# A Performer block with an MLP-Mixer: chunk 0's second channel product and chunk 1's first by seven half-size products, with a new instruction order

## The chip, the cores and the metric

One core of one Trainium2 chip runs the whole program. The metric is the time of one execution on the device in microseconds (us); it is given as a median over the runs shown. TensorE is called PE, VectorE DVE, ScalarE ACT, GpSimd POOL, and SyncE, which here only issues DMAs, SP. PEld is the weight load of PE.

## The reference

Eight batches, eight heads, 576 rows, 64 columns per head, so 512 columns in all. First linear attention with 128 random features, then a Mixer block over the attention's output `x`:

```python
def phi(x):
    proj = np.einsum('bhsd,md->bhsm', x, omega)
    sq = np.sum(x * x, axis=-1, keepdims=True) / 2.0
    h = proj - sq
    h = h - np.max(h, axis=-1, keepdims=True)
    return np.exp(h) / np.sqrt(m)
q_p, k_p = (phi(q_s), phi(k_s))
kv = np.einsum('bhsm,bhsd->bhmd', k_p, v)
z = np.sum(k_p, axis=2)
num = np.einsum('bhsm,bhmd->bhsd', q_p, kv)
den = np.einsum('bhsm,bhm->bhs', q_p, z)[..., None] + 1e-06
...
h = np.maximum(xt @ w_tok1, 0.0) @ w_tok2       # over the 576 rows
u = x + h.transpose(0, 2, 1)
h2 = np.maximum(u @ w_ch1, 0.0) @ w_ch2         # 512 -> 1536 -> 512
return (u + h2).astype(np.float32)
```

## The kernel before

**Tiles.** Each batch's 576 rows are cut into 512 rows, which make one chunk (chunks 0 to 7), and a tail of 64; the eight tails together are chunk 8. For a chunk the attention makes key features `kp` (L707, read out by ACT at L562), query features `qp` (L719), the sums over the keys (L763, L770), and the products with the queries (L796, L798), which DVE (L814) or ACT (L812, head by head) scales by the reciprocals `rc` into `x`. The token mix follows (L824, L831, a relu, L844), and DVE adds the result to `x` at L847: that is `u`, with 128 rows on the partitions. For the channel mix it is needed transposed, as `uT`: chunks from 1 on get it by a DMA that transposes, chunk 0 by PE with an identity.

**The two channel products.** The first product of a chunk takes `uT` and `wc1` (512 by 1536) to `r` (after the relu), the second takes `r` and `wc2` (1536 by 512) to the output rows. Each exists in two forms. The plain first product (L1178; L1184 and L1186 for two column blocks of chunk 0) is 12 column blocks of 4 matmuls with 512 columns. The plain second product, used for chunk 0 alone, is the loop at L1212: 4 row blocks of 12 matmuls with 512 columns, to which L1210 adds `u` by 4 identity matmuls of 128 columns; a copy out (L1218, by the helper at L334) and one store for each row block follow. The fast forms cut each operand into four quarters and do with seven products of quarters what eight would do. They need sums of quarters: for the first product sums of the weights (`qT`, `kT`, `sum`, made once) and sums of `uT`, and joins of the results in `r` (`channel_in_fast`, matmuls L1107, joins L1131 on DVE from pieces that ACT or DVE has read out); for the second product the sums `S` of `r`, the weight differences `T` (L496, made once) and reads that add what is already there (`channel_out_fast`, matmuls L989, reads L969). One fast product of one chunk is 84 matmuls with 256 columns. L343 is the helper `tt` for sums on DVE or POOL, L338 and L340 are the relu on ACT and DVE, and L334 is the copy. Before, the first product is fast from chunk 2 on (`FAST_IN = 2`) and the second from chunk 1 on.

**Loads.** Chunks 0 and 1 are loaded as they are (L367, L378, L385, L399), and PE transposes them. From chunk 2 on a DMA of POOL's queue casts the rows into DRAM scratch and SP's transposing DMA brings them in. `wc1` comes in two halves by L473, the first for column blocks 0 to 5, the second for 6 to 11, and `wc2` in two halves by L488, all by DMAs that POOL issues.

**Order.** Nothing is scheduled while the kernel is built: `ORDER` is a list of job numbers, written out by hand, in which each job (a few instructions on one engine, or a DMA) is issued; a negative number stands for that many warm-up matmuls (L1252, minus one) on PE. `SLOT` gives the buffers and `MOVED` the jobs that run on another engine than the one they are declared for. `Planner.turns` (L163 to L180) looks at jobs with `port=True`: where one on DVE follows one on POOL in the order, or the other way round, the first instruction of the later waits for the last of the earlier. Before, the T sums and the `vbd`, `kt_mask` and `vs` of chunks 0 and 1 were not among them.

Of the kernel before, what the change touches and what calls it, by code (L numbers as in the profile page):

```python
# [213 lines left out]
def kernel(  # L214
# [19 lines left out]
    P = 128  # L234
# [8 lines left out]
    RT = ST // 2  # L243
    RA = R + RT
    NPE = 2
    FAST_IN = 2
    SPLIT = ()
    HALVES = ()
    RW = S * 4 // P
# [205 lines left out]
    def clear(t):  # L455
        return lambda: nc.vector.memset(t, 0.0)
# [829 lines left out]
```

## Time and profile before

| | us |
|---|---|
| median of 3 runs | 269.25 (269.13 to 271.19) |
| the profiled execution: its own time | 270.67 |
| its span in the trace | 268.9 |
| PE busy / PEld busy | 257.9 / 190.6 |
| DVE / ACT / POOL busy | 231.7 / 183.0 / 158.9 |

The span is what the trace covers; the 1.8 us beside it lie before the first and after the last instruction. The profiled execution took 1.4 us more than the median. Busy times are those of the span: an engine that is busy for nearly all of it has little room left, but a matmul's busy time includes the part in which the next has already begun, so PE's share says less than the distance from one matmul's start to the next. The granted clock of PE is full throughout.

### The profile page before, as it was taken

How to read it: one execution, taken by the hardware profiler on the slowest of the kernel's cores; microseconds unless marked ns; L12 is line 12 of the kernel's file. 1: busy time of each engine (PE TensorE's matmuls, PEld its weight loads, DVE VectorE, ACT ScalarE, POOL GpSimd, SP SyncE). 2: the span in 40 equal slices, each digit the busy share in tenths (PEclk: the TensorE clock that was granted, in tenths of full speed). 3: DMA queues.
4: the chain of work that ended last, by engine and by line, in shares of the span. 5: the costliest groups of instructions: out<-in, count | busy, mean ns of one | idle time of the engine just before them, and what ended most of it. 6: DMA issues, size and time to landing. Idle time of an engine off the chain costs nothing.

```text
span 268.9 us, 6989 instructions
## 1 busy us (share of the span) xinstructions
PE 257.9 (96%) x2752; PEld 190.6 (71%) x2752; DVE 231.7 (86%) x494; ACT 183.0 (68%) x425; POOL 158.9 (59%) x160
## 2 busy tenths in 40 slices
PE   4999999999999999989999999999999999999993
PEld 2568455454667985768768777897696788888882
DVE  3999978599999998889999999998987898788982
ACT  1997982089885896879988989878865482273400
POOL 8765553061897966987498852745775004927171
PEclk9999999999999999999999999999999999999999
DMA  7999999999999999999999927844350513040144
GB/s 192 199 208 200 205 207 184 175 220 186 240 168 143 175 207 187 121 198 210 175 222 189 240 85 80 119 85 95 105 152 0 80 67 112 0 157 4 41 146 127
DMA packets 81826, 39.72 MB, mean 148 GB/s; under 512 B 64033, under 2 KB 77729, under 8 KB 81601
## 3 DMA queue, kind: packets, MB, share of 16 engines
q0 software_dynamic: 31712, 17.61, 44.7%
q1 hardware_dynamic: 48560, 19.50, 34.7%
q10 hardware_dynamic: 1520, 2.16, 2.3%
q8 instruction: 21, 0.34, 0.5%
q14 instruction: 13, 0.10, 0.1%
HBM read 35.95 MB, written 16.52 MB: 195 GB/s over the span
## 4 chain that ended last, share of the span: by engine, by line
PE 81%; DMA 7%; POOL 6%; issue 2%; DVE 2%; ACT 1%; POOLq 0%
PE bank L989 23%; PE bank L1107 21%; PE bank L1178 7%; PE bank L1212 4%; PE bank L831 4%; PE bank L844 4%; DMA k<-in_k_dram 4%; DMA uT<-u 3%; PE bank L707 3%; PE bank L796 3%; PE bank L763 2%; PE bank L719 2%; POOL S L343 2%; POOL vs L343 1%; POOL uT L343 1%
## 5 line engine op out<-in xcount | busy, mean ns | idle before, releaser
L562 ACT ACTIVATE kp<-bank 128x512 f16<-128x512 f32 x64 | 35.8, 610 | 13.5 <-PE bank L707 13.1
L338 ACT ACTIVATE r<-bank 128x512 f16<-128x512 f32 (+1 forms) x50 | 29.1, 606 | 20.1 <-PE bank L1107 9.9
L989 PEld LDWEIGHTS <-r 128*128 128x128 f16 x384 | 36.9, 98 | 6.8 <-issue 1.0
L562 ACT ACTIVATE qp<-bank 128x512 f16<-128x512 f32 x64 | 36.7, 631 | 2.5 <-PE bank L719 2.4
L740 DVE TENSOR_REDUCE km<-kp 128x8 f16<-128x1024 f16 x32 | 38.1, 1205 | 0.5 <-ACT kp L562 0.5
L343 POOL TENSOR_TENSOR vs<-v,vs 128x512 f16<-128x512 f16 x22 | 23.7, 1082 | 16.0 <-DVE vs L744 5.5
L1107 PE MATMUL bank<-uT,wc 128*128 128x256 f16 x228 | 30.5, 273 | 1.2 <-DMA uT<-u 1.2
L989 PEld LDWEIGHTS <-S 128*128 128x128 f16 x288 | 27.6, 98 | 4.4 <-POOL S L343 0.2
L1107 PEld LDWEIGHTS <-wc 128*128 128x128 f16 x252 | 23.5, 98 | 5.7 <-DMA uT<-u 1.7
L343 POOL TENSOR_TENSOR S<-r,S 128x768 f16<-128x768 f16 x15 | 24.4, 1641 | 4.5 <-DVE vbd L644 3.4
L989 PE MATMUL bank<-T,r 128*128 128x256 f16 x192 | 23.8, 273 | 0.1
L989 PE MATMUL bank<-T,S 128*128 128x256 f16 x192 | 23.6, 273 | 0.0
L989 PE MATMUL bank<-wc,r 128*128 128x256 f16 x192 | 23.4, 273 | 0.0
L812 ACT ACTIVATE x<-bank,rc 128x64 f16<-128x64 f32 x100 | 22.4, 348 | 0.4 <-DVE rc L803 0.4
L343 POOL TENSOR_TENSOR uT<-uT,uT 128x512 f16<-128x512 f16 x10 | 11.6, 1158 | 17.9 <-PE bank L1107 15.8
L338 ACT ACTIVATE r<-r 128x512 f16<-128x512 f16 (+1 forms) x21 | 16.7, 822 | 7.5 <-DVE r L1131 7.5
L1107 PE MATMUL bank<-uT,qT 128*128 128x256 f16 x126 | 21.7, 272 | 0.0
L847 DVE TENSOR_TENSOR u<-x,bank 128x512 f16<-128x512 f16 x28 | 17.8, 680 | 4.3 <-PE bank L844 4.2
L1107 PE MATMUL bank<-uT,kT 128*128 128x256 f16 x126 | 21.4, 273 | 0.0
L1178 PE MATMUL bank<-uT,wc 128*128 128x512 f16 x88 | 20.5, 380 | 0.0
L969 DVE TENSOR_TENSOR o<-u,bank 128x512 f32<-128x512 f16 x28 | 19.0, 677 | 1.8 <-PE bank L989 1.7
L814 DVE TENSOR_TENSOR x<-bank,rc 128x320 f16<-128x320 f32 x44 | 20.0, 477 | 0.4
(158 smaller groups left out, 612.5 us busy)
## 6 DMA issues: line engine op xcount, KB each, us to landing
out_dram<-o SPq DMA_DIRECT2D x11, 512.0 KB, 4.5
q<-in_q_dram POOLq DMA_DIRECT2D x6, 576.0 KB, 9.2
wc<-in_moe_w_ch_dram POOLq DMA_DIRECT2D x4, 768.0 KB, 13.1
k<-in_k_dram POOLq DMA_DIRECT2D x6, 512.0 KB, 9.4
v<-in_v_dram POOLq DMA_DIRECT2D x6, 512.0 KB, 8.9
out_dram<-o SPq DMA_DIRECT2D x6, 256.0 KB, 3.3
r<-in_q_dram POOLq DMA_DIRECT2D x4, 288.0 KB, 7.6
v<-in_v_dram POOLq DMA_DIRECT2D x4, 256.0 KB, 10.8
```

Source lines behind the costliest of these rows:

```text
L338: nc.scalar.activation(out=out, in_=in_, func=AF.Relu)
L343: (nc.gpsimd if eng == "POOL" else nc.vector).tensor_tensor(**kw)
L562: nc.scalar.activation(out=out, in_=in_, func=AF.Exp, bias=0.0, scale=1.0)
L740: nc.vector.reduce_max(out=t_km[place("km", (b, hp))], in_=src_, axis=AX.X)
L812: nc.scalar.activation(out=to[:, j], in_=ps[:, j], func=AF.Copy, scale=rc[:, j : j + 1])
L814: nc.vector.tensor_tensor(out=to, in0=ps, in1=rc.unsqueeze(2).broadcast_to((P, NJ + 1, D)), op=ALU.mult)
L831: nc.tensor.matmul(ps, w1m[:, j, tb * P : (tb + 1) * P], x[:, j, :], start=False, stop=(j == NJ - 1))
L847: nc.vector.tensor_tensor(out=t_u[place("u", b)][:, j, :], in0=t_x[place("x", b)][:, j, :], in1=bank(n), op=ALU.add)
L969: nc.vector.tensor_tensor(out=o, in0=a, in1=ps, op=ALU.add)
L989: nc.tensor.matmul(ps[:, j * DH : (j + 1) * DH], a[:, cb, j * P : (j + 1) * P], w[:, cb, :], start=(bank_of(b, j0) not in held and j == j0 ...
L1107: nc.tensor.matmul(ps[:, n, :], w(a)[:, (2 * m + n) * P : (2 * m + n + 1) * P], x_[:, a], start=(what in ("P1", "P2", "P5") and n == 0 and ...
L1178: nc.tensor.matmul(ps, wc1[:, db, cb * P : (cb + 1) * P], moving(db), start=(db == 0), stop=(db == ND - 1))
```

## The change

`FAST_IN` goes from 2 to 1, so chunk 1's first product takes the fast form; the loop at L1212 goes, so chunk 0's second product does. Chunk 0 has no `u` with rows on the partitions kept for its reads: four of its reads are therefore plain copies, and `rows_into` adds `u` on PE by 20 identity matmuls of 128 columns; where a product is shared by two quarters, one set has a negative identity (`minus16`, made once on DVE). Its output goes in 2 stores in place of 4, in the same layout. The first two heads' keys are read out one head at a time (two jobs in place of one). The T sums, `vbd`, `kt_mask`, `qt_dup` and `vs` now have `port=True` for every chunk. The copy of the transposed `omega` may run on another engine. `ORDER`, `SLOT` and `MOVED` are new in full. Lines of the kernel after are 4 to 23 higher than before (L1009 is the second product's matmul, L1129 the first's, L999 `rows_into`, L347 `tt`, L504 the T sums).

```diff
-    FAST_IN = 2
+    FAST_IN = 1
+    minus16 = sb([P, P], FP16, "minus16")
+    def minus_identity():
+        nc.vector.tensor_scalar(out=minus16, in0=ident16, scalar1=-1.0, scalar2=None, op0=ALU.mult)
+    j_minus = add("DVE", 0.2, -2.0, minus_identity, deps=[j_ident])
...
-        j_T.append(add("DVE", 0.95, KEYS["T"], ..., deps=[*j_wc2, *j_T[-1:]]))
+        j_T.append(add("DVE", 0.95, KEYS["T"], ..., deps=[*j_wc2, *j_T[-1:]], port=True))
...
-            j_ktm = add("DVE", 0.15, kkt + 0.01, kt_mask, ..., port=b >= 2)
+            j_ktm = add("DVE", 0.15, kkt + 0.01, kt_mask, ..., port=True)
-            j_v = add(e_vs, 1.07, ..., vs_, ..., port=b >= 2)
+            j_v = add(e_vs, 1.07, ..., vs_, ..., port=True)
...
+            plain = c == 0 and base
...
-                if e_read == "ACT":
-                    nc.scalar.copy(out=o, in_=ps)
+                if plain:
+                    copy(e_read, o, ps)
                     return
...
+        rest = {1: [(0, 0, ident16)], 3: [(1, 1, ident16)], 5: [(0, 1, ident16), (1, 1, minus16)], 6: [(1, 0, ident16)]}
+        def rows_into(ps, i, e, by):
+            for j in range(2):
+                for d in range(2):
+                    nc.tensor.matmul(ps[:, j * DH + d * P : j * DH + d * P + P], t_uT[place("uT", 0)][:, 2 * i + j, 2 * e + d, :], by,
+                                     start=False, stop=False, skip_group_check=True)
...
+                    for x in rest.get(k, []) if c == 0 else []:
+                        rows_into(ps, *x)
...
-        if fast:
-            channel_out_fast(c, key, jr)
-            return
-        for j in range(NJ):
-            n = ("h4", c, j)
...
+        channel_out_fast(c, key, jr, jt)
 
     for i in range(4):
-        transposes(0, 2 * i, 2 * i + 2, HEAD["kx"][i], ...)
+        for h0 in (0, 1) if i == 0 else (2 * i,):
+            transposes(0, h0, h0 + 1 if i == 0 else h0 + 2, HEAD["kx"][i], ...)
...
 ORDER = [
-    2, 38, 16, 3, 7, 6, 4, 9, 12, 10, 0, -8, 41, 1, 14, 39, 42, 40, 47, 48, 8, 11, 13, 21, 22, 19, 17, 5, 78, 49,
...
+    17, 2, 7, 5, 6, 4, 12, 10, 8, 23, 0, 9, 13, 31, 20, 11, 18, 32, 19, 29, 22, 3, 1, 39, -8, -7, -6, 48, 40, 50,
...
```

POOL issues the loads one after the other, and at the program's head it also makes the 128x128 identity (the two rows `masks.py`). First before, then now (`r` here are buffers for loaded rows, `vt` and `v` the values, `w` the token weights):

```order
L378 DMA r_129<-in_k_dram 64x1x512
L399 DMA vt_93<-in_v_dram 128x1x128
L367 DMA r_129<-in_q_dram 128x1152 x2
masks.py:197 MEMSET S 128x128
masks.py:199 ISA
masks.py:199 AFFINE_SELECT S<-S 128x128
L399 DMA vt_93<-in_v_dram 128x1x128
```

```order
L382 DMA r_130<-in_k_dram 64x1x512
L371 DMA r_130<-in_q_dram 128x1152 x2
L403 DMA vt_94<-in_v_dram 128x1x128
L371 DMA r_131<-in_k_dram 128x1152
masks.py:197 MEMSET S 128x128
masks.py:199 ISA
masks.py:199 AFFINE_SELECT S<-S 128x128
L403 DMA vt_94<-in_v_dram 128x1x128
```

Five DMAs stand ahead of the identity in place of four. Some rows later in the same engine come the channel weights; `v_91` before and `v_92` now are the values of chunk 1, in two halves:

```order
L473 DMA wc_80<-in_moe_w_ch_dram 128x4x768
L399 DMA vt_94<-in_v_dram 128x1x128 x2
L681 COPY qpt_107<-qpt_107 128x8x64
L473 DMA wc_80<-in_moe_w_ch_dram 128x4x768
L488 DMA wc_81<-in_moe_w_ch_dram 128x6x512
L385 DMA v_91<-in_v_dram 128x4x256 x2
L488 DMA wc_81<-in_moe_w_ch_dram 128x6x512
```

```order
L389 DMA v_92<-in_v_dram 128x4x256
L471 DMA S<-in_moe_w_tok_dram 64x256
L371 DMA r_131<-in_q_dram 128x1152
L371 DMA r_131<-in_k_dram 128x1152
L626 COPY T<-mask 128x16
L347 TENSOR_TENSOR T<-vt_94,mask 128x16x64
L389 DMA v_92<-in_v_dram 128x4x256
L403 DMA vt_95<-in_v_dram 128x1x128
L692 COPY qpt_108<-qpt_108 128x8x64
L481 DMA wc_81<-in_moe_w_ch_dram 128x4x768 x2
L403 DMA vt_95<-in_v_dram 128x1x128
L496 DMA wc_82<-in_moe_w_ch_dram 128x6x512 x2
```

Both halves of those values now stand ahead of both halves of `wc1`, and stood behind them.

On DVE the place is chunk 1's attention output (`x_119` before, `x_120` now) and the weight differences `T`. First before, then now:

```order
L814 TENSOR_TENSOR x_119<-bank_69,rc_148 128x5x64
L343 TENSOR_TENSOR kT_89<-wc_80 128x768
L496 TENSOR_TENSOR T<-wc_81 128x1536
L340 TENSOR_SCALAR r_122<-bank_65 128x512
L847 TENSOR_TENSOR u_123<-x_119,bank_69 128x512
L847 TENSOR_TENSOR u_123<-x_119,bank_64 128x512
L847 TENSOR_TENSOR u_123<-x_119,bank_65 128x512
L847 TENSOR_TENSOR u_123<-x_119,bank_67 128x512
L496 TENSOR_TENSOR T<-wc_81,T 128x1536
L496 TENSOR_TENSOR T<-wc_81 128x1536
L334 COPY o_131<-bank_66 128x512
```

```order
L504 TENSOR_TENSOR T<-wc_82 128x1536
L814 RECIPROCAL rc_143<-bank_68 128x5
L504 TENSOR_TENSOR T<-wc_82,T 128x1536
L814 RECIPROCAL rc_144<-bank_64 128x5
L504 TENSOR_TENSOR T<-wc_82 128x1536
L814 RECIPROCAL rc_146<-bank_66 128x5
L504 TENSOR_TENSOR T<-wc_82,T 128x1536
L814 RECIPROCAL rc_147<-bank_65 128x5
L814 RECIPROCAL rc_148<-bank_63 128x5
L825 TENSOR_TENSOR x_120<-bank_66,rc_146 128x5x64
```

Three of the four T sums came behind chunk 1's `x`, two of them behind its `u`; all four now stand ahead of the `x` scales.

On PE the place is the end of chunk 3's token mix for the tails (`64x512`) and the start of the next first product. Before:

```order
L898 MATMUL bank_63<-r_121,w_79 64x512
L898 LDWEIGHTS w_79
L898 MATMUL bank_63<-r_122,w_79 64x512
L1107 LDWEIGHTS wc_80
L1107 MATMUL bank_68<-uT_127,wc_80 128x256
```

and now:

```order
L909 MATMUL bank_68<-r_122,w_80 64x512
L909 LDWEIGHTS w_80
L909 MATMUL bank_68<-r_123,w_80 64x512
L1009 LDWEIGHTS r_130
L1009 MATMUL bank_66<-T,r_130 128x256
```

Before, chunk 3's first product followed at once; now 24 matmuls of chunk 2's second product, 4 matmuls for queries (2 with 256 columns, 2 with 512) and 18 for keys come between.

More of the change, by code (lines that the diff above doesn't have):

```diff
@@ L129 @@
+    1398: "ACT", 1399: "ACT", 1408: "DVE", 1419: "DVE", 1429: "DVE", 1431: "ACT", 1433: "POOL", 1435: "POOL",
+    1437: "POOL", 1438: "POOL", 1439: "POOL", 1456: "ACT", 1462: "POOL", 1463: "POOL", 1464: "POOL", 1468: "DVE",
+    1480: "ACT", 1484: "DVE", 1495: "ACT", 1496: "ACT", 1500: "DVE", 1505: "DVE", 1512: "ACT", 1514: "POOL",
+    1516: "POOL", 1520: "POOL", 1549: "ACT", 1550: "SP", 1551: "POOL", 1552: "POOL", 1553: "ACT", 1554: "SP",
+    1559: "ACT", 1560: "SP",
 }
@@ L501, with om_out @@
                 deps=[j_om16, j_ident], take=[("bank", "om")])
-    j_omT = add("DVE", 0.2, -9.0, lambda: nc.vector.tensor_copy(out=omT, in_=bank16("om")[:, 0:P]), deps=[j_omt], give=[("bank", "om")])
+    e_omT = engine("DVE")
+    def om_out():
+        copy(e_omT, omT, bank16("om")[:, 0:P])
+    j_omT = add(e_omT, 0.2, -9.0, om_out, deps=[j_omt], give=[("bank", "om")])
     def rows_of(b, w):
@@ L649, in kt_mask @@
                 )
-            j_ktm = add("DVE", 0.15, kkt + 0.01, kt_mask, deps=[j_ktm, j_msk], take=take_vbd, give=[("kmt", b)], port=b >= 2)
+            j_ktm = add("DVE", 0.15, kkt + 0.01, kt_mask, deps=[j_ktm, j_msk], take=take_vbd, give=[("kmt", b)], port=True)
             def vbd():
@@ L970, in read @@
             return add(e_read, 0.345 * (j1 - j0), key + KEYS["c2"] + step * k, go, deps=deps, take=[o_tag(i)],
-                       give=([("bank", bank_of(b, j0))] if free else []) + ([("u", c)] if base and c < B else []))
+                       give=([("bank", bank_of(b, j0))] if free else []) + ([("u", c)] if base and 0 < c < B else []))
         def late_base(k, i, e, x, deps):
@@ L1170, in channel_mix @@
         jr = [None] * NCB
-        fast = c >= NPE - 1
-        order = [x for i in range(NH) for x in (i, i + NH)] if fast else range(NCB)
+        order = [x for i in range(NH) for x in (i, i + NH)]
         for pos, cb in enumerate(order):
```

99 lines of the change are left out of this document (37 added, 62 removed), and 148 rows, old and new, of the table ORDER.

## The prediction

> **What bounds the kernel now.** I read the shares first, then the chain that ended last, then the stretches.
>
> ```profile
> PE 257.9 (96%) x2752; PEld 190.6 (71%) x2752; DVE 231.7 (86%) x494; ACT 183.0 (68%) x425; POOL 158.9 (59%) x160
> PE 81%; DMA 7%; POOL 6%; issue 2%; DVE 2%; ACT 1%; POOLq 0%
> 20.00:40.00 20.00, 20.00 (x245) 12.24 (x242) 17.61 (x41) 17.28 (x41) 10.09 (x13) 1.00 1.25 204
> 40.00:60.00 20.00, 20.00 (x176) 10.13 (x171) 15.60 (x32) 7.61 (x20) 6.59 (x9) 1.00 1.20 198
> 60.00:80.00 20.00, 20.00 (x186) 10.92 (x185) 18.51 (x46) 17.59 (x41) 13.42 (x14) 1.00 1.07 199
> 80.00:100.00 20.00, 20.00 (x249) 17.14 (x247) 19.18 (x43) 16.05 (x44) 16.64 (x17) 1.00 1.16 174
> 100.00:130.00 30.00, 27.97 (x323) 21.02 (x321) 26.22 (x55) 24.46 (x61) 22.65 (x22) 1.00 1.28 185
> 130.00:160.00 30.00, 30.00 (x339) 21.94 (x338) 28.63 (x60) 26.46 (x68) 23.24 (x22) 1.00 0.95 182
> ```
>
> The first two lines are the busy shares and the chain by engine. The six rows are stretches: length, then busy time of PE, PEld, DVE, ACT and POOL, then clock, DMA share and GB/s. PE is on 81% of the chain and busy without a gap in 20 to 100 us; only 100 to 130 lacks 2 us. So PE work that is saved early shortens the run, as long as PE then finds something ready. But DVE is busy 17.61 + 15.60 + 18.51 + 19.18 + 26.22 + 28.63 = 125.75 of the 140 us from 20 to 160. It has 14.25 us to spare, 5.89 of them in 40 to 80, where both changed products run. The question is whether a saving on PE survives a second engine that is nearly full.
>
> **PE: the products.** The distance between matmuls comes from runs of one line in the chain (start, us, line, count):
>
> ```profile
> 43.39 2.59 PE bank L1212 x12
> 53.10 0.22 PE bank L1210 x4
> 60.07 4.42 PE bank L1178 x20
> 76.30 1.31 PE bank L989 x12
> 128.47 3.95 PE bank L1107 x36
> L989 PEld LDWEIGHTS <-r 128*128 128x128 f16 x384 | 36.9, 98 | 6.8 <-issue 1.0 <-DVE r L340 0.2
> ```
>
> A 512-column matmul takes 2.59 / 12 = 0.216 us (4.42 / 20 = 0.221), a 256-column one 1.31 / 12 = 0.109 (3.95 / 36 = 0.110), an identity matmul 0.055. Each of the two products loses 48 x 0.216 = 10.37 us and gains 84 x 0.109 = 9.16: 1.21 saved, twice 2.42. The residual takes 20 identity matmuls for 16, +0.22. PE's sum is **-2.2 us**. Two more warm-up matmuls lie in PE's idle head and count nothing; without that cover they cost 0.43.
>
> The weight loads, 98 ns each in the last row, seem to speak against it: 168 in place of 96. But 12 products with 12 loads of their own take 1.31 us, so the loads run beside the matmuls. Here the Trainium skill has a rule against the change: "TensorE: Matmul & The Clock Gate", section "Measured speedup vs the span model", says that a weight load overlaps a running matmul only where the two use different row groups, and these use all rows. By that rule each half-size matmul would take 109 + 98 ns and each full one 216 + 98, the two products 168 x 0.207 - 96 x 0.314 = +4.6 us in place of -2.42; the 1.31 us row disagrees, as 12 would take 2.48.
>
> **PE: two waits at 100 and 117 us.** Start, length, line, count, and the idle time before it with its releaser:
>
> ```profile
> 101.37 0.29 PE L599 MATMUL bank<-omT,kT 64*128 64x128 f16 x4 [0.70 <-DMA kT<-k]
> 115.58 0.62 PE L898 MATMUL bank<-r,w 128*64 128x512 f16 x4
> 117.41 0.61 PE L1107 MATMUL bank<-uT,wc 128*128 128x256 f16 x4 [1.21 <-DMA uT<-u]
> ```
>
> At 117.41 the first product of chunk 3 waits 1.21 us for its transposed `u`, right behind L898. In the new order 24 matmuls of the second product (2.6 us at 0.109), 4 for queries (0.65) and 18 for the key sums come between, over 3.2 us. Unless `u` itself is that much later, the wait goes: -1.21, bounds 0 and -1.21. The 0.70 is a transposing DMA that waits on the loads; the order moves its use back a little, so I take half, -0.35, bounds -0.70 and +1.21 (as long a wait as the other transposing DMA's). Together **-1.56**. Late next is DVE, below.
>
> **The head.** PE's first work waits for the identity that POOL makes after its DMA issues:
>
> ```profile
> 2.74 1.14 POOL L367 DMA_DIRECT2D r<-in_q_dram  x2
> 4.16 0.29 POOL masks.py:199 TENSOR_SCALAR_AFFINE_SELECT S<-S 128x128 f32<-128x128 f32 x1
> 4.51 1.11 PE L518 MATMUL bank<-S,wc 128*128 128x128 f32 x4 [2.71 <-POOL S masks.py:199]
> ```
>
> L518 begins as soon as the identity is there. Five issues in place of four stand ahead of it now, so it comes one issue of L367 later, 1.14 / 2 = **+0.57** (bounds 0, if ACT's chain from the first keys sets the head anyway, and 0.57). Reading out the first keys one head at a time lets ACT begin earlier by at most one of its pieces, 0.6 us, but it then has one more instruction; I give it nothing.
>
> **The weights' landing.** All these loads stand in POOL's queue.
>
> ```profile
> L473 POOL DMA_DIRECT2D wc<-in_moe_w_ch_dram x2: 757/780/804, 14.0 to 18.6; - x2
> DMA to landing us min/median/max: 11.4/11.6/11.9
> 27.72 2.76 PE L1178 MATMUL bank<-uT,wc 128*128 128x512 f16 x12
> v<-in_v_dram POOLq DMA_DIRECT2D x4, 256.0 KB, 10.8
> ```
>
> The two halves of `wc1` are issued at 14.0 and 18.6 and land 11.4 to 11.9 us later, at about 25.9 and 30.0. The first product starts at 27.72. In the new order two value loads of 256 KB stand ahead of both: 524 KB at the 204 GB/s of the row for 20 to 40 is 2.6 us, so they land near 28.5 and 32.6, earlier issue or not, since bandwidth and not issue holds them back. The first half is then needed at 28.3; the fourth column block, which needs the second half, is about 3 us of PE work later, near 31.4. One wait of at most 1.2 us, some of it already in the start of the head: I take **+0.8**, bounds 0 and +2.6. `wc2` lies behind both in either order and keeps its place.
>
> **DVE, ACT and POOL.** The counts are those of the program's order, the durations those of the rows:
>
> ```profile
> L1131 DVE TENSOR_TENSOR r<-r,bank 128x512 f16<-128x512 f32 x21 | 14.0, 678 | 1.6 <-PE bank L1107 1.3 <-ACT r L334 0.2
> L969 DVE TENSOR_TENSOR o<-o,bank 128x512 f32<-128x512 f32 x21 | 14.0, 675 | 0.9 <-PE bank L989 0.8
> L340 DVE TENSOR_SCALAR r<-bank 128x512 f16<-128x512 f32 x11 | 7.4, 678 | 2.4 <-PE bank L831 1.8 <-PE bank L1178 0.4
> L340 DVE TENSOR_SCALAR r<-r 128x1024 f16<-128x1024 f16 x12 | 5.2, 459 | 0.1
> L343 DVE TENSOR_TENSOR S<-S,r 128x768 f16<-128x768 f16 x14 | 7.7, 553 | 0.2
> L814 DVE TENSOR_TENSOR x<-bank,rc 128x320 f16<-128x320 f32 x44 | 20.0, 477 | 0.4
> L812 ACT ACTIVATE x<-bank,rc 128x64 f16<-128x64 f32 x100 | 22.4, 348 | 0.4 <-DVE rc L803 0.4
> L496 DVE TENSOR_TENSOR T<-wc 128x1536 f16<-128x1536 f16 x2 | 1.9, 949 | 0.0
> L343 POOL TENSOR_TENSOR S<-r,S 128x768 f16<-128x768 f16 x15 | 24.4, 1641 | 4.5 <-DVE vbd L644 3.4 <-DVE S L343 0.6 <-DVE r L340 0.5
> L343 POOL TENSOR_TENSOR vs<-v,vs 128x512 f16<-128x512 f16 x22 | 23.7, 1082 | 16.0 <-DVE vs L744 5.5 <-DMA v<-in_v_dram 3.4 <-DVE r L343 2.4
> ```
>
> DVE gains 9 joins x 0.678 = 6.1, 3 adding reads x 0.675 = 2.0, 4 relus of 1024 from buffers x 0.459 = 1.8 and 6 of 512 at half of that, 1.4, 4 more copies out of PSUM at the joins' 0.68 = 2.7, and 8 sums of `uT`, of `r` and of weights at 0.553 = 4.4. It loses 8 relus from PSUM x 0.678 = 5.4, 5 `x` scales x 0.477 = 2.4 that go to ACT, 2 `vs` that go to POOL and five other copies at 0.68 (4.8). Net 18.4 - 12.6, about **+6 us** of DVE work, nearly all between 20 and 100 us. ACT gains 25 pieces of `x` x 0.348 = 8.7, and its copies gained and relus lost about cancel; the 12.4 us that it has free in 40 to 60 hide that, and without this cover the relus would come later by as much. POOL gains 4 sums net at 1.64 and 2 `vs` at 1.08, 8.7 us; it was busy 6.59 of 20 in 40 to 60: hidden too. The four T sums, contiguous now, stand ahead of chunk 1's five `x` scales. That chunk's `u` thereby comes 3 x 0.95 us later in DVE's order than it would, which is what the freed scales (2.4) about give back. What of the +6 reaches PE is bounded by 0 (the 5.89 us idle in 40 to 80 takes all) and +6 (the idle stays where it is, in front of work that PE releases). I take 0 for the likeliest, because the row for 40 to 60 is the emptiest of all, and the price stands in the rival below.
>
> **Turns.** The waits between DVE and POOL now hold in chunks 0 and 1 too. Behind a waiting T sum stand the `x` scales and so `u`; behind a waiting POOL sum stand the DMA issues for later chunks.
>
> ```profile
> L343 POOL TENSOR_TENSOR vs<-v,vs x22: 1056/1061/1496, 36.8 to 196.8; 128x512 f16<-128x512 f16 x22
> L343 POOL TENSOR_TENSOR T<-vt,T 128x1024 f16<-128x1024 f16 x1 | 1.9, 1922 | 0.7 <-DVE T L644 0.7
> ```
>
> Without turns a POOL operation was stretched by 1496 - 1061 = 0.44 us at most; with them a T sum may wait for a whole POOL product, 1.92. Bounds -0.44 and +1.9; I take **+0.44**, the nearer row. The Trainium skill, "SBUF — State Buffer", section "Who interferes with whom", says that a DVE operation with two SBUF inputs and a POOL operation that reads SBUF exclude each other for the whole instruction in any case: by that a turn would cost nothing but the choice of who goes first, 0 in place of 0.44. The stretch to 1496 agrees with some exclusion, and is shorter than a whole one.
>
> **The sum.** On the profiled execution: 270.67 - 2.20 - 1.56 + 0.57 + 0.80 + 0.44 = 268.72. That execution was 1.42 above the median, so 267.3.
>
> **The rivals.**
>
> *DVE becomes the bound* (slower). Place: 40 to 80 us, DVE at 34.11 of 40 before. If the idle time sits in front of instructions that PE releases, it cannot be filled, and two thirds to all of the 6 us (4 to 6) reaches PE: 271.3 to 273.3, middle 272.3. It decides from where DVE is busy over 39 of those 40 us. For it: 19.18 of 20 already in 80 to 100, so nothing is made up there. Against: PE has work of two other chunks to put in between, and ACT has 12 us free. Chance 0.25.
>
> *All is recovered*: both waits go (-1.91), the head and the landing cost nothing: 270.67 - 2.20 - 1.91 = 266.56, less 1.42 gives 265.1. For it: a new order can place what I priced as waits behind other work. Against: DVE. Chance 0.23.
>
> *The landing takes it*: the second half of `wc1` costs the full 2.6: 269.1, no change. For it: 204 GB/s is as much as the queue moves in any stretch here. Against: 3 us of column blocks come first. Chance 0.08.
>
> *The weight loads bind*, so that the change does not do what it says: 270.67 + 4.6 + 0.22 - 1.42 = 274.1. Against it the 1.31 us row. Chance 0.02.
>
> **How the numbers follow.** The likeliest, **267.3 us**, has 0.42 and 265.7 to 269.0 of its own. One per cent, 2.7 us, is about what a measurement of this kernel can tell from no change, as the three runs spread over 2.1. Below 266.56 lie 0.17 of the forecast and all of the recovery, 0.40; above 271.9 lie two thirds of the DVE rival and the weight loads, 0.18; between them 0.42. The range from 264.4 to 272.4 leaves out the better end of the recovery and the worse half of the DVE rival, under 0.2 together.
>
> **What would show it.** Each fast product as runs of 12 at 1.31 us, in chunks 0 and 1 too; L518 near 5.1 us; no wait of the first product behind L909; the first column block of the first product starting within 28 to 29 us. DVE over 39 of 40 us in 40 to 80, with PE waiting for DVE's joins or `x`, would show the rival. The forecast is wrong if PE gets gaps before 100 us, which it had none of, or if the waits at 100 to 120 only move to another chunk.

## The result and the profile after

| | us | to before on the same chip |
|---|---|---|
| after, median of 4 runs | 273.04 (272.92 to 273.18) | 1.0126 [1.0077, 1.0176], before 269.57 |
| after, again on another chip | 273.63 | 1.0167 [1.0126, 1.0209], before 269.35 |
| profiled execution, before and after | 270.67 and 273.02 | span 268.9 and 271.2 |

The change is slower by 1.3 to 1.7%. Forecast were 267.3 us and 264.4 to 272.4. Here and below the medians hold every execution, and the ratios leave out those that took over 1.5% longer than the fastest of the same kernel (one each of h3 and h5, two of h4).

The shares and the chain by engine, then the stretches as in the prediction (length, busy PE, PEld, DVE, ACT, POOL, clock, DMA share, GB/s), of after:

```profile
PE 260.8 (96%) x2830; PEld 199.5 (74%) x2830; DVE 236.2 (87%) x509; ACT 190.1 (70%) x456; POOL 166.8 (61%) x166
PE 89%; ACT 4%; DVE 3%; POOL 2%; issue 1%; POOLq 0%; DVEq 0%
20.00:40.00 20.00, 19.56 (x254) 12.20 (x252) 16.49 (x42) 17.94 (x46) 9.90 (x13) 0.93 1.24 209
40.00:60.00 20.00, 19.91 (x215) 13.43 (x215) 18.71 (x41) 13.32 (x38) 8.43 (x7) 1.00 0.98 147
60.00:80.00 20.00, 19.91 (x238) 15.27 (x239) 19.16 (x47) 19.12 (x49) 14.90 (x18) 1.00 1.07 198
100.00:130.00 30.00, 30.00 (x353) 22.98 (x351) 28.98 (x63) 24.64 (x57) 23.35 (x25) 1.00 1.14 173
```

Three things are new: PE is no longer full in 20 to 100 us, its clock was 0.93 in 20 to 40, and 100 to 130 is full. DVE went from 34.11 to 37.87 of the 40 us from 40 to 80.

Busy shares hide how much PE loses, so I took every matmul's start from the trace. A matmul of this kernel needs 0.216 us for 512 columns, 0.109 for 256 and some 0.056 for 128 at full clock, by the rows of the prediction. For one with 64 rows I count half of that and for one in f32 twice; this is a way of counting, not a measurement, and as both kernels have equally many of these it cancels in the differences. What the distance to the next start has beyond that is **lost time**: waiting, or a slow clock. By stretch, in us:

| | before | after | h3 | h8 | t2 |
|---|---|---|---|---|---|
| PE's own work | 244.9 | 243.2 | 242.8 | 242.8 | 243.2 |
| lost, 0 to 40 | 10.5 | 15.2 | 11.2 | 11.5 | 14.1 |
| lost, 40 to 100 | 1.8 | 3.6 | 8.9 | 5.8 | 3.4 |
| lost, 100 to 130 | 3.5 | 1.4 | 1.4 | 1.3 | 1.6 |
| lost, later | 2.7 | 2.9 | 3.2 | 2.9 | 2.9 |

The last three columns are experiments below. For after against before: -1.7 + 4.7 + 1.8 - 2.2 + 0.2 = +2.8 up to the start of the last matmul; what follows it is 0.45 shorter, and 2.35 is the 2.3 us by which the spans differ. PE got what was promised, 1.7 of work and 2.2 of waits, and lost 6.5 in the first 100 us. The 4.7 up to 40 us divide into -0.6 up to 14 us, +4.1 from 14 to 24 and +1.3 from 24 to 40.

**The products.** Pieces of after's chain (start, us, what):

```profile
33.08 1.02 PE bank L1199 x4
47.99 2.78 PE bank L1009 x24
53.16 1.48 PE bank L1009 x12
56.37 1.31 PE bank L1009 x12
```

The half-size matmuls keep their distance of 0.109 us (1.31 / 12) in chunk 0 too. But the first product starts at 33.08 in place of 27.72, and the second product of chunk 0 at 47.99 in place of 41.91. What follows this second start takes 223.2 us of the span in after and 227.0 before: the change loses 6.1 us ahead of it and gains 3.8 behind it.

**The waits at 100 and 117 us.** PE's instructions in order of time, after:

```profile
116.70 0.62 PE L909 MATMUL bank<-r,w 128*64 128x512 f16 x4
117.26 1.48 PE L1009 MATMUL bank<-T,r 128*128 128x256 f16 x12
```

Nothing waits behind L909 now; at 100 us no idle time is left either. That is not shown to be the new order's doing: in h2 and p1 below, which have before's order there and a span 7 and 3 us longer, PE waits for neither DMA either. Coming later was enough.

**The head.** PE's clock in stretches of 2 us (columns as above), the first two rows of before, the others of after; then three pieces of after's chain and one row each of its ACT and PE:

```profile
16.00:18.00 2.00, 1.87 (x35) 1.25 (x34) 2.00 (x6) 2.00 (x5) 1.12 (x2) 1.00 1.19 211
20.00:22.00 2.00, 2.00 (x40) 1.94 (x37) 1.85 (x9) 1.69 (x7) 2.00 (x3) 1.00 1.12 205
14.00:16.00 2.00, 0.95 (x17) 0.29 (x9) 1.10 (x3) 2.00 (x7) 1.77 (x2) 1.00 1.30 201
16.00:18.00 2.00, 1.38 (x14) 0.68 (x14) 1.88 (x6) 2.00 (x6) 1.75 (x3) 1.00 1.26 203
18.00:20.00 2.00, 1.87 (x25) 1.22 (x23) 1.75 (x3) 2.00 (x6) 0.76 (x2) 0.81 1.32 206
20.00:22.00 2.00, 2.00 (x13) 0.90 (x11) 1.05 (x4) 1.75 (x5) 2.00 (x3) 0.50 1.12 206
22.00:24.00 2.00, 1.91 (x42) 1.57 (x40) 1.65 (x6) 1.30 (x7) 1.84 (x4) 0.83 1.41 185
```

```profile
5.02 1.11 PE bank L529 x4
12.65 1.20 PE bank L1249 x5
20.05 1.71 PE bank L1249 x4
13.88 0.62 ACT L622 ACTIVATE kpt<-bank,kt_nb 128x128 f16<-128x128 f32 x2 [1.44 <-PE bank L1249]
16.08 0.28 PE L680 MATMUL bank<-qT,omT 64*128 64x256 f16 x2 [0.67 <-ACT qT L338]
```

The identity comes at 5.02, as forecast (before 4.51). What is late lies behind it: of the five warm-up matmuls at 12.65 one goes into the bank that holds the scores of the tails' keys, and ACT's exp of them waits 1.44 us for it. PE then finds work for only 0.95 and 1.38 of 2 us, its clock stands at half for 3.4 us (the rows from 18 to 24 show its parts), and four warm-up matmuls that should take 4 x 0.216 = 0.86 us take 1.71 in the chain. Every wait of PE between 14 and 18 us is for ACT; the longest is the last row above. Before, ACT is busy for all 12 us from 8 to 20; in after it is busy for 10.05 of them, and its idle time lies before 14. So PE follows ACT there, and ACT has lost some 2 us by 14. How much of the time the halved clock costs is open: one of the four executions of after had the full clock throughout and took 273.18 us, no less than the others.

**DVE ahead of chunk 1's `u`**, in order of time, after:

```profile
43.71 0.95 DVE L504 TENSOR_TENSOR T<-wc 128x1536 f16<-128x1536 f16 x1
46.66 0.92 DVE L504 TENSOR_TENSOR T<-wc,T 128x1536 f16<-128x1536 f16 x1
48.78 1.68 DVE L825 TENSOR_TENSOR x<-bank,rc 128x320 f16<-128x320 f32 x4
52.09 1.01 DVE L347 TENSOR_TENSOR S<-S,r 128x768 f16<-128x768 f16 x2
55.19 2.48 DVE L858 TENSOR_TENSOR u<-x,bank 128x512 f16<-128x512 f16 x4
```

The four T sums (the first and last are shown) fill 43.7 to 47.6, the scales follow, then the sums `S` for the second product, then `u`. PE hardly waits for this in after, because its own second product comes so late.

### The profile page after: what moved, and what is told of

It reads as the page before. It is cut to its first block, busy times and chain, and to the rows that moved or that the text cites. A ratio compares the mean times of both kernels' runs of the same rounds, so it can differ in the third digit from the quotient of the medians.

```text
span 271.2 us, 7205 instructions
## 1 busy us (share of the span) xinstructions
PE 260.8 (96%) x2830; PEld 199.5 (74%) x2830; DVE 236.2 (87%) x509; ACT 190.1 (70%) x456; POOL 166.8 (61%) x166
## 4 chain that ended last, share of the span: by engine, by line
PE 89%; ACT 4%; DVE 3%; POOL 2%; issue 1%; POOLq 0%; DVEq 0%
PE bank L1009 30%; PE bank L1129 26%; PE bank L842 5%; PE bank L855 5%; PE bank L774 3%; PE bank L1199 3%; PE bank L718 3%; PE bank L807 3%; PE bank L730 3%; PE bank L529 1%; PE bank L1249 1%; PE bank L835 1%; ACT qp L573 1%; PE bank L893 1%; PE bank L895 1%
## 5 line engine op out<-in xcount | busy, mean ns | idle before, releaser
L1009 PEld LDWEIGHTS <-r 128*128 128x128 f16 x432 | 41.4, 98 | 7.9 <-issue 1.6
L1129 PE MATMUL bank<-uT,wc 128*128 128x256 f16 x264 | 36.3, 273 | 0.0
L1009 PEld LDWEIGHTS <-S 128*128 128x128 f16 x324 | 31.1, 98 | 5.8 <-issue 0.7
L347 POOL TENSOR_TENSOR vs<-v,vs 128x512 f16<-128x512 f16 x24 | 25.0, 1056 | 13.0 <-DVE r L344 5.5
L823 ACT ACTIVATE x<-bank,rc 128x64 f16<-128x64 f32 x125 | 28.3, 345 | 3.3 <-DVE rc L814 3.3
L1129 PEld LDWEIGHTS <-wc 128*128 128x128 f16 x288 | 27.5, 98 | 3.7 <-issue 0.2
L347 POOL TENSOR_TENSOR S<-r,S 128x768 f16<-128x768 f16 x16 | 26.0, 1642 | 4.2 <-DVE S L347 4.1
L1009 PE MATMUL bank<-T,r 128*128 128x256 f16 x216 | 26.9, 273 | 0.0
L1009 PE MATMUL bank<-T,S 128*128 128x256 f16 x216 | 26.5, 273 | 0.0
L1009 PE MATMUL bank<-wc,r 128*128 128x256 f16 x216 | 26.4, 273 | 0.1
L1129 PE MATMUL bank<-uT,qT 128*128 128x256 f16 x144 | 25.3, 273 | 0.0
L1129 PE MATMUL bank<-uT,kT 128*128 128x256 f16 x144 | 25.0, 273 | 0.0
L347 POOL TENSOR_TENSOR r<-r 128x768 f16<-128x768 f16 x10 | 16.3, 1638 | 11.5 <-DVE r L347 9.6
L338 ACT COPY qp<-bank 128x512 f32<-128x512 f32 x21 | 12.4, 600 | 11.1 <-PE bank L1129 10.0
L1153 DVE TENSOR_TENSOR r<-r,bank 128x512 f16<-128x512 f32 x24 | 16.2, 676 | 2.4 <-PE bank L1129 2.0
L347 POOL TENSOR_TENSOR uT<-uT 128x512 f16<-128x512 f16 x9 | 10.4, 1155 | 12.7 <-DVE r L344 12.7
```

Source lines behind the costliest of these rows:

```text
L347: (nc.gpsimd if eng == "POOL" else nc.vector).tensor_tensor(**kw)
L823: nc.scalar.activation(out=to[:, j], in_=ps[:, j], func=AF.Copy, scale=rc[:, j : j + 1])
L1009: nc.tensor.matmul(ps[:, j * DH : (j + 1) * DH], a[:, cb, j * P : (j + 1) * P], w[:, cb, :], start=(bank_of(b, j0) not in held and j == j0 ...
L1129: nc.tensor.matmul(ps[:, n, :], w(a)[:, (2 * m + n) * P : (2 * m + n + 1) * P], x_[:, a], start=(what in ("P1", "P2", "P5") and n == 0 and ...
L1153: nc.vector.tensor_tensor(out=r3(i, j, m), in0=kept(what, m).rearrange("p (n t) -> p n t", n=2), in1=pair(b, m), op=ALU.add)
```

## The experiments

Most kernels here are after (or before) with a stretch of the other's order of jobs, buffers and engines put in; where two orders meet (the seam), new waits can arise, and I name them. The head is the program's start, up to chunk 0's first or second product; "old head" is before's order.

**The head alone, both ways.** h1 has before's order on all engines up to the first product, then after's; h2 is before with after's order up to there. POOL's loads, h1 against after:

```diff
-v_92 (chunk 1's values, first half), ..., v_92 (second half), ..., wc_81 x2, ..., wc_82 x2
+wc_81, vt_95 x2, COPY qpt, wc_81, wc_82, v_92 x2, wc_82
```

> The kernel after, but every job up to chunk 0's first channel product in the order, on the engines and in the buffers of before (identity, loads, transposes, chunk 0's attention and token mix); from there on the order of after. Theory 'head': the loss arises before the first L1199 (27.72 us before, 33.08 after), by PE waits and a lower clock there, and the rest of the new order keeps its gains: first product near 28 us, 268.0 to 269.5 us in all. Rival 'DVE is the bound' (40 to 80 us, DVE 37.9 of 40 busy after): an earlier head is lost in waits behind DVE, 271.5 to 273.

> The kernel before (plain products in chunk 0 and chunk 1 as they were), but every job up to chunk 0's first channel product in the order, on the engines and in the buffers of after. Theory 'head': first product near 33 us, 273 to 275 us. Rival 'DVE is the bound': before's DVE has 5.9 us free in 40 to 80 and takes the late head in, 269.5 to 271.

Measured: h1 277.43, 1.0306 [1.0254, 1.0359]; h2 278.38, 1.0332 [1.0274, 1.0390]. Both were slower than either parent. In h1 the first product started at 30.01, but one DVE row shows what the seam did:

```profile
35.35 0.69 DVE L359 TENSOR_TENSOR vs<-v,vs 128x512 f16<-128x512 f16 x1 [6.83 <-DMA v<-in_v_dram]
```

After's later order needs chunk 1's values early, and before's loads bring them late. In h2 the first product started only at 37.45, later than in either parent. Neither run says what the head alone is worth.

**The same without that seam.** x1 keeps after's order on POOL (two halves of chunk 1's keys exchanged) and has before's order on the other engines up to the first product; x2 is h1 with chunk 1's values ahead of `wc1` and the halves of `wc1` exchanged.

```diff
 DMA r_131<-in_q_dram 128x1152
+DMA v_92<-in_v_dram 128x4x256 x2
 DMA wc_81<-in_moe_w_ch_dram 128x4x768
 ...
-DMA v_92<-in_v_dram 128x4x256 x2
```

> The kernel after; PE, DVE, ACT and SP work through chunk 0's token mix stands in the order, on the engines and in the buffers of before, POOL's loads stand as after (but the two halves of chunk 1's keys change places), and the rest is the order of after. The first run of this kind lost 4.1 us where DVE waited at 35 us for chunk 1's values, which the old load order brings late; here they come early. Theory 'head': first product near 28.5 us, 268.0 to 270 us in all. Rival 'DVE is the bound': 271.5 to 273.

> As the run with the old head, loads in the old order too, but chunk 1's two value loads moved ahead of the channel weights, and the two halves of wc1 exchanged, as after has them. The identity then stands behind four DMA issues as before. Theory 'head': no wait of DVE at 35 us, 267.5 to 270 us; the identity 0.5 us earlier than in the other run with old compute order. Rival 'DVE is the bound': 271.5 to 273. If the weights' landing is what counts: the first product starts late, near 29 to 30, with PE waiting for wc, and the time is 270 to 272.

Measured: x1 275.96, 1.0258 [1.0218, 1.0297]; x2 273.95, 1.0190 [1.0156, 1.0224]. The first product started at 34.93 and 33.66. In x1 PE waits 1.35 us for DVE's `vs` (18.41) and 2.06 us for a load of keys (23.35). In x2, POOL and PE:

```profile
16.94 0.74 POOL L493 DMA_DIRECT2D wc<-in_moe_w_ch_dram  x1 [1.43 <-DMA r<-in_k_dram]
20.20 0.62 POOL L704 COPY qpt<-qpt 128x512 f16<-128x512 f16 x1
20.88 0.20 PE L821 MATMUL bank<-kvsb,qpt 128*128 128x65 f16 x1 [2.33 <-POOL qpt L704]
```

POOL's DMA issues wait here until earlier transfers have landed (1.43 us in the first row), and a copy that PE needs stands behind them. In h1, where the two loads stand later, the copy runs at 17.44 and PE has no such wait: two loads moved forward cost PE 2.33 us through POOL, not through their landing. So the head is a balance of loads and ACT, DVE and POOL work, and half of one does not go with half of the other.

**The warm-ups.** w1 puts the fifth matmul into another bank; w2 leaves the five out.

```diff
-    138, 122, 100, 42, 43, 15, 84, -2, -2, -2, -2, -4, 66, 74,
+    138, 122, 100, 42, 43, 15, 84, -2, -2, -2, -2, -2, 66, 74,
```

> The kernel after with one number of the order changed: the last of the five warm-up matmuls at 12.6 us goes into bank 1, as the four before it, in place of bank 3, whose key scores for the tails L622 has yet to read. Theory 'head': ACT's wait of 1.44 us at 13.88 goes, its work up to the first product comes earlier by most of it, PE idles less in 14 to 18 us and the clock drops for a shorter time: 270.5 to 272. Rival 'DVE is the bound': 273, no change.

> The kernel after without the five warm-up matmuls at 12.6 us. ACT's wait goes as with the other bank, but PE has 1.1 us less work in the stretch after which its clock was halved (18.8 to 22.7 us). Theory 'head', with the idle PE as the cause of the low clock: the clock drops as early or earlier, and the time is 0.3 to 1 us above that of the run with the other bank, 271 to 273. If the clock has another cause: the same as with the other bank or better, 270.5 to 272.

Measured: w1 272.56, 1.0107 [1.0067, 1.0146]; w2 273.13, 1.0135 [1.0092, 1.0178]. In w1 the clock stayed at 1.00, in all six executions. In w2 it was at half for 6.8 us:

```profile
18.00:20.00 2.00, 2.00 (x16) 0.53 (x12) 1.91 (x5) 1.95 (x6) 2.00 (x3) 0.50 1.34 207
```

By the ratios w1 is 0.5 us faster than the first run of after and 1.6 faster than the second; the intervals overlap, so the bank and the halved clock together cost at most something like this. The starts of the first product say no more: 32.70 in w1 and 34.07 in w2, but 33.08 and 34.30 in the two profiled executions of after itself, since a load of keys made PE wait up to 1.4 us near 9 us in some executions and not in others. What the five warm-ups are worth in time is not shown.

**The turns.** n1 takes `port=True` away from the T sums, `qt_dup` and the `vbd`, `kt_mask` and `vs` of chunks 0 and 1.

```diff
-  ... deps=[*j_wc2, *j_T[-1:]], port=True))
+  ... deps=[*j_wc2, *j_T[-1:]]))
-  ... give=[("v", b)], port=True)
+  ... give=[("v", b)], port=b >= 2)
```

> The kernel after with the flag for turns as before: the T sums, vbd, kt_mask, qt_dup and vs of chunks 0 and 1 take none. If the turns cost what was put down for them, 0.4 us: 272.6. If they are part of the loss in the head: POOL's wait of 2.0 us for DVE at 35.8 and the like go and 271 to 272 comes out. If they save contention: 273.0 to 273.6.

Measured 276.01, 1.0254 [1.0199, 1.0308], so by 0.9 to 1.3% slower than after by the ratios, though its interval overlaps that of after's second run: the turns cost nothing that shows. One T sum took 2.28 us here and POOL's S sums 2.23 on average, where after has 0.96 and 1.63. But the loss is not there: the second product starts at 50.30, and what follows takes 223.5 us, against 223.2 in after. It lies in the head, and whether the turns or the chance of the loads made it is not shown.

**Everything up to chunk 0's second product as before.** h3 has before's order up to there and after's behind it, where PE's late start cannot hide DVE; h4 is before with after's order up to there. h3 against after, on DVE: before's head, and the T sums behind only two of the five `x` scales of chunk 1.

```diff
+TENSOR_TENSOR x_120 x2
 TENSOR_TENSOR kT, qT x2
 TENSOR_TENSOR T x4
-TENSOR_TENSOR x_120 x5
+TENSOR_TENSOR x_120 x3
```

> The kernel after, with everything up to chunk 0's second product in the order, on the engines and in the buffers of before, and everything from there on (both fast products, the new order) as after. The traces put the second product's start at 41.9 us before and 48.0 after, and what follows at 227.0 and 223.2 us of span. Theory 'head': 42 to 43 plus 223 to 225, that is a span of 265 to 268 and 267 to 270 us, below before. Rival 'DVE is the bound' in 40 to 100 us: it cannot use the earlier start, 271.5 to 273.5.

> The kernel before (plain products), with everything up to chunk 0's second product in the order, on the engines and in the buffers of after, and everything from there on as before. Theory 'head': 48 plus 227, 275 to 277 us. Rival 'DVE is the bound': the later start is taken in by DVE's free 5.9 us, 269.5 to 271.5.

> The kernel after once more, on the same chip as the other runs of this call, to compare them with: 272.5 to 273.5 us.

Measured: h3 275.49, 1.0228 [1.0194, 1.0261]; h4 280.79 and 284.95 in the two executions that the ratio counts, 1.0502 [1.0428, 1.0577]; after 273.63, 1.0167 [1.0126, 1.0209]. The profile of h4 is of an execution of 538.85 us and isn't read. In h3, PE and DVE:

```profile
43.94 2.78 PE L1030 MATMUL bank<-wc,r 128*128 128x256 f16 x24
50.32 0.39 PE L856 MATMUL bank<-x,w1t 64*128 64x512 f16 x2 [3.38 <-DVE x L846]
47.66 0.95 DVE L525 TENSOR_TENSOR T<-wc,T 128x1536 f16<-128x1536 f16 x1
48.89 1.28 DVE L846 TENSOR_TENSOR x<-bank,rc 128x320 f16<-128x320 f32 x3
```

The second product starts 4 us earlier than in after, and PE then waits 3.38 us for `x`, which stands behind the T sums. Behind that wait the clock stands at half for 3.4 us (51.0 to 54.4), about 1.7 us more. The lost time moved from before 40 us (15.2 to 11.2) to behind it (3.6 to 8.9), and what follows the second product's start takes 228.5 us in place of 223.2. So there is a second bound right behind the head. With the late head and after's order behind it, it never shows: in the second run of after, w1, w2, n1, t2, x1, x2 and h1, where that start lies between 46.89 and 51.22, the rest takes 223.2 to 223.5 us.

**Moving the T sums.** t1 is after with the T sums behind chunk 1's scales; h5 is h3 with them there and four weight sums behind the S sums; h6 is h5 with two T sums ahead of the S sums, two behind, and without their turn; h7 is h6 with two copies of output and one scale on ACT. p1 is the other way round: before, with all four T sums ahead of the last four scales.

```diff
 (t1, h5)
-TENSOR_TENSOR T x4
 TENSOR_TENSOR x_120 ...
+TENSOR_TENSOR T x4
 TENSOR_TENSOR S
 (p1)
+TENSOR_TENSOR T x4
 TENSOR_TENSOR x_119 x4
-TENSOR_TENSOR T x4 (one here, two behind u, one later)
```

> The kernel after with one edit: the four T sums stand behind chunk 1's last x scale on DVE in place of ahead of the scales. Theory 'two bounds': the scales come 3.7 us earlier, but PE gets to the second product only at 48 because of the head, and no more than 0.5 us is gained: 272.5 to 274. Theory 'the row of T sums is the cause by itself': 270 to 271.5.

> The kernel after with everything up to the second product as before, as in the run that gained nothing by it, and on DVE besides the four T sums and four weight sums moved from ahead of chunk 1's last three x scales to behind them (the weight sums behind the S sums). There PE waited 3.5 us at 46.7 for those scales. Theory 'two bounds, one behind the other' (a late head, and DVE's row of T sums ahead of x): both are gone, the wait at 46.7 too, a span of 266 to 269 and 268 to 271 us. Theory 'head alone' or 'DVE's amount of work alone': DVE has as much to do as before the move, 272 to 275.5.

> The kernel before with one edit: the four T sums stand ahead of chunk 1's last four x scales on DVE, as the new order has them. PE's first matmul of the token mix (45.98 us) needs those scales and stands in front of PE's other work; they come up to 3.7 us later. Theory 'two bounds': 271.5 to 273.5. If DVE or PE make it up later: 269 to 270.

> As the run with the old order until the second product and the T sums behind the x scales, where PE then waited 4.9 us at 49 for the S sums, because POOL's two S sums stood waiting (5.1 us) for their turn behind the T sums. Here the T sums take no turn, and only two of the four stand ahead of the S sums. Theory 'two bounds and the turn': POOL's S sums run from 44.6 to 47.9 beside the T sums, PE's wait falls to 1 us or less, 270.5 to 272.5 us. Theory 'DVE's amount of work' (DVE has no idle time from 39 to 61 us in any order): a wait of PE as long turns up at the next thing that DVE makes, 274 to 276.5.

> The same, with two copies out of chunk 0's second product and one x scale given from DVE to ACT (which is idle for 6 of 10 us there): 1.8 us less work on DVE in 44 to 60 us. Theory 'two bounds and the turn': the same time as without it, within 0.7 us. Theory 'DVE's amount of work': 1 to 1.8 us shorter than without it.

Measured: t1 282.70, 1.0480 [1.0431, 1.0528]; h5 276.52, 1.0242 [1.0199, 1.0285]; p1 273.52, 1.0123 [1.0088, 1.0157]; h6 275.70, 1.0272 [1.0242, 1.0302]; h7 278.85, 1.0392 [1.0372, 1.0411]. One row each of PE in p1 and h5, of POOL and PE in t1, and of POOL and DVE in h6:

```profile
48.66 0.39 PE L821 MATMUL bank<-x,w1t 64*128 64x512 f16 x2 [2.68 <-DVE x L811]
54.08 2.31 PE L1030 MATMUL bank<-T,S 128*128 128x256 f16 x10 [4.90 <-DVE S L368]
56.05 3.22 POOL L345 TENSOR_TENSOR S<-r 128x768 f16<-128x768 f16 x2 [12.02 <-DVE minus L458]
60.86 1.46 PE L1007 MATMUL bank<-T,S 128*128 128x256 f16 x6 [5.96 <-DVE S L345]
44.92 3.24 POOL L368 TENSOR_TENSOR S<-r 128x768 f16<-128x768 f16 x2
46.56 2.43 DVE L525 TENSOR_TENSOR T<-wc 128x1536 f16<-128x1536 f16 x1
```

p1 is the cleanest: nothing of before is changed but the place of the T sums, PE waits 2.68 us for `x`, its clock then stands at half for 3.4 us (49.2 to 52.6, about 1.7 us more), and the kernel is 3.3 us slower by the ratio and 4.1 by the medians, about as much as by the whole change. Behind the scales they do no better: in h5 and t1 POOL's S sums get their turn only after them, and PE waits 4.90 and 5.96 us for S in place of `x`. Without the turn (h6) the sum that meets POOL's S takes 2.43 us. h7 has PE's `T,S` product at 50.70 in place of 51.58, but one of the copies then stood behind other work of ACT, and this cost more than it gained, so it shows nothing on the amount of DVE's work.

**Leaving the T sums out**, with the old head (h8, else h3) and with the new one (t2, else after): the four sums are not computed, and slices of the weights stand in their place. Four kernels make a square of head and T sums.

```diff
-    T1, T2, T3, T4 = [t_T[:, i] for i in range(4)]
+    T1, T2, T3, T4 = W12, W22, W22, W21
-  add("DVE", 0.95, KEYS["T"], lambda o=out_, a=a, b=b: nc.vector.tensor_tensor(...), ..., port=True)
+  add("DVE", 0.95, KEYS["T"], lambda: None, ...)
```

> The kernel after with everything up to chunk 0's second product in before's order (as in h3), and with the four T sums left out: slices of the weights stand in for them, so the operands of every fast second product that would be T are not computed. Theory of two bounds (the head is 5 to 6 us late, and behind it DVE has about 6 us of work more ahead of chunk 1's u): with the early head it is DVE that is late, so the 3.8 us of T sums show: PE's wait of 3.5 us ahead of chunk 1's query weights shrinks to under 1.5, chunk 1's products start at least 3 us earlier than in h3, and the time is h3's 275.5 less 3 to 5, 270.5 to 272.5. Head alone (only the late head matters, DVE fills anyway): no change from h3, 275 to 276. DVE amount alone: h3 less 3.8, and the same 3.8 in t2.

> The kernel after as it is, with the four T sums left out in the same way (slices of the weights stand in for them). Theory of two bounds: with the late head the second product's start and not DVE sets the time, so less comes back than in h8: after's time less 0 to 1.5, 272 to 273.6. DVE amount alone (the second engine is full in 40 to 80 us, whatever the head does): after less about 3.8, 269.5 to 270.2, that is no slower than before by more than half a per cent. Head alone: no change from after, 273 to 274.

Measured:

| | with T sums | without |
|---|---|---|
| new head | 1.0126 [1.0077, 1.0176] and 1.0167 [1.0126, 1.0209] | 1.0180 [1.0135, 1.0225], 273.84 us |
| old head | 1.0228 [1.0194, 1.0261], 275.49 us | 1.0071 [1.0040, 1.0102], 270.92 us |

With the old head the T sums cost 1.57% of 269 us, 4.2 us; with the new one nothing that shows. The traces agree: what follows the second product's start takes 228.5 us in h3 and 225.0 in h8, but 223.2 in after and 223.3 in t2. The stretch from 40 to 60 us, h3 and then h8:

```profile
40.00:60.00 20.00, 16.08 (x164) 11.00 (x163) 17.73 (x39) 6.69 (x20) 10.32 (x10) 0.91 0.97 145
40.00:60.00 20.00, 17.71 (x196) 12.34 (x194) 17.33 (x40) 9.87 (x27) 14.45 (x15) 1.00 1.25 172
```

PE does 32 matmuls more there, and its clock is 1.00 in place of 0.91: about 1.7 of the 4.2 us are the clock that fell behind the wait. That is two bounds, one behind the other, and neither DVE's amount alone (the gain would be the same in both rows) nor the head alone (there would be none). Without the T sums the head by itself is worth the step from 1.0071 to 1.0180, 2.9 us. But h8 still loses 4.0 us more than before in 40 to 100, without any T sum.

**One half of the change.** k1 keeps chunk 0's second product plain and before's order to its end; chunk 1's first product is fast, and the rest is after's.

```diff
-        channel_out_fast(c, key, jr, jt)
+        if c == 0:
+            for j in range(NJ): ...   # the plain loop of before
+            return
+        channel_out_fast(c, key, jr, jt)
```

> One half of the change alone: chunk 0's second product stays plain (48 matmuls of 512 columns, copies, four stores) and everything up to its end keeps before's order, so three T sums stay behind chunk 1's x scales as before and the fourth goes behind chunk 1's first joins; chunk 1's first product is fast, and from there on the order is after's, turns included. Theory of two bounds (the head, and the T and S sums ahead of chunk 1's u): neither bound is touched here, so PE keeps 1.21 us of the one fast product and the 2.2 us of the two waits between 100 and 130 us, less up to 1 us of new waits where the two orders meet: 266 to 268 us, ratio 0.985 to 0.997. Theory that any added DVE work before 100 us reaches PE (9 joins and 6 halves of relu, some 7 us, are still there): PE gets gaps of 2 us or more between 55 and 80 us and the time is 269.5 to 272. Theory that the new turns cost: no better than before, without such gaps.

Measured 278.44, 1.0369 [1.0341, 1.0397]: far from the expectation. DVE's last output copy waited for PE until 59.73, and behind it, in after's order, stood weight sums, a maximum and the tails' adds, before the `uT` sums that the fast product needs at 67.01; PE lost 11.1 us in 40 to 100. That is the seam's doing in good part, so the run doesn't show what half of the change is worth with an order of its own. It does show again that the fast form puts several short DVE operations between `uT` and its first useful matmul, and that they wait behind whatever is ahead of them. No kernel tried was faster than before.

## Why the prediction was wrong

- **PE's sum, -2.2.** Right: -1.7 measured, in which the two extra warm-ups (0.43) count as work; they lie in the wait for the identity, as forecast.
- **The weight loads.** They did not bind: 12 half-size matmuls take 1.31 us in after too (56.37), not 2.48. The sentence of the Trainium skill that the prediction goes by stands in "TensorE: Matmul & The Clock Gate", section "The mechanism"; that section also lets loads into a background weight buffer run ahead.
- **The waits at 100 and 117 us, -1.56.** Both went, -2.2, but the reason that I gave, the work put in between, is not shown: they go in h2 and p1 too, with before's order there. The number may be luck.
- **The identity, +0.57.** It came 0.51 later, but PE's lost time up to 14 us, with warm-ups counted as work, is no larger than before (-0.6), so nothing of this is seen in the end.
- **The rest of the head** is the step that failed first. I wrote "I give it nothing" of the first keys and took PE's idle head as free cover. In the measured kernel the head loses 4.7 us, 4.1 of them from 14 to 24 us, where PE first waits for ACT and then runs at half clock. "ACT's chain from the first keys", which I had only as the reason for a bound of 0, is what PE follows there. The new order moves many instructions of the head, and I had priced three things of it. The first product at 33.08, not "within 28 to 29 us", is the sign I had named. By w1 the bank and the halved clock are 0.5 to 1.6 of it; why ACT is late for the rest is open, as the mixed heads (h1, x1, x2) brought waits of their own.
- **The landing of `wc1`, +0.8.** Nothing: in after the first product waits 0.29 us for DVE's `uT` and for no weights. The halves were issued at 19.8 and 20.6 and landed 9.1 to 12.0 us later, by 32.6, near the forecast; the product came so late that they were there. (204 GB/s is not the most that was moved: 2 us of before's head have 298.)
- **DVE's +6 us, taken at 0.** The second failed step. I called 40 to 60 us the emptiest stretch, but the work falls ahead of chunk 1's `u`, in one serial piece: the T sums, `x`, S, `u`. p1 prices the place of the T sums alone at 3.3 us, h8 against h3 at 4.2, some 1.7 of each being the clock that falls behind the wait. The amount was over-estimated: +4.5 us of DVE in all. Averages over 20 us said nothing about that.
- **The turns, +0.44.** They cost nothing that shows; n1, without them, is not faster than after.
- **The DVE rival** gave 271.3 to 273.3, and the time is in it. Its mechanism is there, but not as I put it: DVE is busy 37.87 of 40 us and not over 39, and in after itself 3.8 us less of DVE's work brings nothing (t2). That the time lies in its range is luck. The head sets the time, and DVE would if the head did not.

The sum was 268.72 for the profiled execution, which took 273.02, +4.3. The head gave +4.1 more than the identity's term (4.7 - 0.57), 40 to 100 us +1.8, later stretches +0.2 and PE's work with the warm-ups +0.5; the waits gave -0.6, the landing -0.8, the turns -0.4 (what they do is in the stretches) and the shorter end -0.4: 4.4, with rounding.

## What to carry to other kernels

A saving on the bounding engine has to be checked against the serial chain of small operations that its faster form needs first (sums of operands, reads, scales), instruction by instruction at the place where they stand; the share of idle time of the second engine over 20 us is no cover. Where an order is new in full, price the milestones of the head (first product, second product, `u`) from the trace before believing in local gains; here everything behind the second product took the same 223 us whatever was done to the late head. And when a bound is taken away and the time stays, look for the next bound right behind it with a two-by-two of both, since either alone can show no gain.

## What the hardware showed

- PE's clock halved without a long pause. In after no PE wait between 14 and 18 us is over 0.67 us, but PE was busy 2.33 of 4 us, and the clock then stood at 0.50 for 3.4 us. The Trainium skill, "TensorE: Matmul & The Clock Gate", section "What's actually happening", speaks of an idle window of some 3.4 us; the length agrees, but here a thinly filled stretch was enough. The busy share does not tell when: in h6 PE was busy 1.88 of the 4 us from 48 to 52, and the clock stayed at 1.00.
- A wait of PE can thus cost more than its length: in p1 2.68 us of waiting were followed by 3.4 us at half clock, about 1.7 us more.
- A DVE sum of two SBUF operands beside POOL's sums took 2.43 us in place of 0.95 (h6): it began at 46.56, POOL's two sums ended at 48.16, and 48.16 + 0.95 is near its end at 48.99. That is the whole exclusion of the Trainium skill, "SBUF — State Buffer", "Who interferes with whom", which my forecast had held to be partial. In n1 both sides show it: a T sum and two of POOL's S sums are each longer by about what the other still had to run. Turns choose who goes first; where the choice is wrong they hold POOL for up to 12 us (t1).
